# A branch hint for the jump past the general path, at the head of each engine's instructions

## The chip, the cores and the metric

The kernel runs on one core of one Trainium2 chip. The metric is the device time of one execution in microseconds (us); the number that counts is the median of several executions.

## What is computed

Two parts follow each other. The first is a gated linear attention over `B = 4` batches, `H = 8` heads, `S = 768` steps and head size `D = 48`, all in float32. Per head and step, with a state matrix of 48 by 48:

```
y[t]  = r[t] . (state + u * k[t] (x) v[t])
state = w[t] * state + k[t] (x) v[t]
```

The second takes the heads side by side as rows of 384 numbers and runs a gated block:

```
h = relu(x @ w_in)                      # 384 -> 1024
u, v = h[:, :512], h[:, 512:]
v_n = (v - mean(v)) / sqrt(var(v) + 1e-6)
v_s = w_spatial @ v_n + b_spatial       # over the 768 steps
out = (u * v_s) @ w_out                 # 512 -> 384
```

## The kernel before

The sequence is cut into chunks of 128 steps, six for each of the four batches, so 24 slots. In each slot decay products are formed by two scans on VectorE, the chunk's scores and outputs by matrix products on TensorE, and the state is carried to the next chunk. Behind each slot one normalised part of the gated block (`hv_unit`) runs, and behind each batch its gate and output parts (`g_unit`, `out_unit`). Products that must be exact to float32 are made of three passes over split operands (`mm3`, lines 582 to 584).

None of this is a loop on the chip: every instruction of the fast path is written out, which makes thousands for TensorE and some hundreds for each other engine. The order is written by hand. `PLAN` is a list of 1810 entries; each names an engine (T TensorE, V VectorE, A ScalarE, G GpSimd, S SyncE for the transfers) and an operation, and five entries (F) are idle matmuls that keep TensorE at work. `issue` (line 713) walks the list and issues each entry on its engine. Nothing on the chip decides about the order.

The chunked form divides by products of decays, so it holds only while these are not too small and no decay is above 1. `range_check` (lines 792 to 802) reduces that to one integer, `bad`, in the last entries of the plan. Behind the plan every engine loads `bad` from memory into a register (line 849), and a branch on each engine (line 850) decides: when `bad` is 1, a slow step by step form runs, `general()`, which lies in the program between the branch and the end; when it is 0, as with these inputs, every engine jumps past it. Behind the jump the engines clear their semaphores, meet, and end.

The last output tile is copied by ScalarE (line 708) and stored by a transfer that SyncE issues (line 710); it lies ahead of SyncE's load of `bad`.

## Time and profile before

| what | us |
|---|---|
| median of three runs | 373.29 |
| lowest and highest of them | 369.5 and 373.3 |
| the profiled execution, its own time | 369.84 |
| span of the profiled execution, first to last instruction | 368.0 |
| TensorE busy | 353.6 (96% of the span) |
| VectorE, ScalarE, GpSimd busy | 252.5, 176.6, 164.5 |

The profiled execution's own time is 1.8 us above its span. Of three runs one took 369.5 and two took 373.3, so an execution can differ from another by 1% with nothing changed, and the profiled one is of the short kind. In the profile PE is TensorE, PEld its weight loads, DVE VectorE, ACT ScalarE, POOL GpSimd and SP SyncE; a name with a q (SPq) is that engine's instruction queue, where register, branch, semaphore and transfer-issuing instructions run. Those are not counted as busy.

### The profile page before, as it was taken

How to read it: one execution, taken by the hardware profiler on the slowest of the kernel's cores; microseconds unless marked ns; L12 is line 12 of the kernel's file. 1: busy time of each engine (PE TensorE's matmuls, PEld its weight loads, DVE VectorE, ACT ScalarE, POOL GpSimd, SP SyncE). 2: the span in 40 equal slices, each digit the busy share in tenths (PEclk: the TensorE clock that was granted, in tenths of full speed). 3: DMA queues.
4: the chain of work that ended last, by engine and by line, in shares of the span. 5: the costliest groups of instructions: out<-in, count | busy, mean ns of one | idle time of the engine just before them, and what ended most of it. 6: DMA issues, size and time to landing. Idle time of an engine off the chain costs nothing.

```text
span 368.0 us, 9503 instructions
## 1 busy us (share of the span) xinstructions
PE 353.6 (96%) x3824; PEld 327.5 (89%) x3824; DVE 252.5 (69%) x475; ACT 176.6 (48%) x470; POOL 164.5 (45%) x211
## 2 busy tenths in 40 slices
PE   7897899999999999999999999999999999999992
PEld 7786688989998898999889999999899998999991
DVE  5989998979977986678756785885784562422240
ACT  3565778745334776614363856422256257303111
POOL 4878866446434753448644305265342220233030
PEclk9999989999999999999999999999999999999998
DMA  7988567822365447324355644242345101100102
GB/s 201 304 246 228 193 210 218 247 61 69 111 177 170 135 132 219 111 89 139 106 166 169 185 122 132 89 138 85 119 137 157 63 2 45 62 4 0 67 0 75
DMA packets 33013, 47.70 MB, mean 130 GB/s; under 512 B 3264, under 2 KB 21824, under 8 KB 32960
## 3 DMA queue, kind: packets, MB, share of 16 engines
q1 hardware_dynamic: 32960, 47.00, 43.2%
q8 instruction: 32, 0.52, 0.6%
q14 instruction: 21, 0.17, 0.1%
HBM read 42.27 MB, written 4.72 MB: 128 GB/s over the span
## 4 chain that ended last, share of the span: by engine, by line
PE 84%; DVE 7%; POOL 2%; issue 2%; DMA 1%; SPq 1%; ACT 0%; POOLq 0%; DVEq 0%; ACTq 0%
PE pyw L502 9%; PE pv L582 9%; PE pv L584 8%; PE pv L583 8%; PE pa L462 6%; PE po L582 5%; PE po L584 5%; PE po L583 5%; PE pu L582 4%; PE ph L582 4%; PE pu L584 4%; PE pu L583 4%; PE ph L583 4%; PE ph L584 4%; PE pd L540 2%; PE pt L482 2%
## 5 line engine op out<-in xcount | busy, mean ns | idle before, releaser
L582 PE MATMUL pv<-ws,vh 128*128 128x384 f32 x192 | 65.5, 341 | 0.0
L584 PE MATMUL pv<-ws,vl 128*128 128x384 f32 x192 | 64.5, 336 | 0.8 <-POOL vl L654 0.8
L583 PE MATMUL pv<-ws,vh 128*128 128x384 f32 x192 | 64.3, 335 | 0.0
L690 POOL TENSOR_TENSOR t<-t,us 128x384 f32<-128x384 f32 x21 | 22.7, 1088 | 56.1 <-DVE t L688 56.0
L467 DVE COPY_PREDICATED As<-mask,pa 128x512 f32<-128x512 int32 x48 | 34.5, 734 | 11.3 <-PE pa L462 5.6
L692 ACT CAST gh<-t 128x384 fp32r<-128x384 f32 x32 | 16.0, 511 | 48.5 <-POOL t L690 36.3
L688 DVE TENSOR_TENSOR t<-pv,b_sb 128x384 f32<-128x384 f32 x32 | 17.6, 553 | 28.6 <-PE pv L584 28.6
L582 PEld LDWEIGHTS pv<-ws,vh 128*128 128x128 f32 x192 | 36.1, 188 | 1.1 <-DVE prod L408 0.2
L584 PEld LDWEIGHTS pv<-ws,vl 128*128 128x128 f32 x192 | 36.0, 188 | 1.1 <-POOL vl L654 1.1
L583 PEld LDWEIGHTS pv<-ws,vh 128*128 128x128 f32 x192 | 36.1, 188 | 0.3
L443 POOL TENSOR_SCALAR_AFFINE_SELECT As<-dg 128x512 f32<-128x512 f32 x33 | 24.9, 762 | 23.9 <-DVE dg L428 10.9
L404 DVE TENSOR_TENSOR_SCAN F<-zz,W 112x512 f32<-112x512 f32 x24 | 29.2, 1218 | 8.6 <-ACT zz L416 6.5
L582 PE MATMUL pu<-xT,wi 128*128 128x384 f32 x96 | 33.1, 344 | 0.0
L582 PE MATMUL po<-wo,gh 128*128 128x384 f32 x96 | 33.1, 344 | 0.0
L584 PE MATMUL pu<-xT,wi 128*128 128x384 f32 x96 | 32.3, 337 | 0.0
L584 PE MATMUL po<-wo,gl 128*128 128x384 f32 x96 | 32.3, 337 | 0.0
L583 PE MATMUL po<-wo,gh 128*128 128x384 f32 x96 | 32.2, 336 | 0.0
L583 PE MATMUL pu<-xT,wi 128*128 128x384 f32 x96 | 32.2, 336 | 0.0
L462 PE MATMUL pa<-rr,kk 48*128 48x128 f32 x384 | 27.9, 284 | 3.1 <-POOL As L443 1.6
L654 POOL TENSOR_TENSOR vl<-hv,vh 128x512 fp32r<-128x512 f32 x14 | 20.7, 1484 | 22.2 <-ACT vh L652 11.9
L582 PE MATMUL ph<-wi,xT 128*128 128x512 f32 x72 | 29.7, 413 | 0.6 <-DVE S L548 0.6
L412 DVE TENSOR_TENSOR_SCAN pa<-zz,W 112x512 f32<-112x512 f32 x24 | 29.3, 1222 | 0.3
(182 smaller groups left out, 842.6 us busy)
## 6 DMA issues: line engine op xcount, KB each, us to landing
N<-in_nat_dram SPq DMA_DIRECT2D x18, 384.0 KB, 3.4
Nw<-in_gt_dram SPq DMA_DIRECT2D x16, 384.0 KB, 3.4
W<-in_tr_dram SPq DMA_DIRECT2D x24, 224.0 KB, 3.4
kk<-in_tr_dram SPq DMA_DIRECT2D x24, 224.0 KB, 4.0
rr<-in_tr_dram SPq DMA_DIRECT2D x24, 224.0 KB, 3.7
v<-in_nat_dram SPq DMA_DIRECT2D x24, 192.0 KB, 2.9
out_dram<-ot SPq DMA_DIRECT2D x24, 192.0 KB, 1.9
wst<-in_w_spT_dram SPq DMA_DIRECT2D x12, 192.0 KB, 4.3
```

What stands on the lines that cost most here:

```text
L404: op({"V": 1.24}, lambda: nc.vector.tensor_tensor_scan(flat(F()[:R])[:, ::-1], flat(zz[:R])[:, ::-1], flat(W())[:, ::-1], 0.0, ALU.max, AL ...
L412: op({"V": 1.24}, lambda: nc.vector.tensor_tensor_scan(flat(E()[:R]), flat(zz[:R]), flat(W()), 0.0, ALU.max, ALU.mult), r=[(W, 0), ("zz", ...
L443: e.affine_select(out=As(), in_=dg()[:, j::2].unsqueeze(2).broadcast_to([P, G, C]), pattern=[[0, G], [1, C]], compare_op=ALU.is_equal, fil ...
L462: nc.tensor.matmul(pa[j]()[:, g, :], kk()[rs, g, :], rr()[rs, g, :], start=True, stop=True)
L467: op({"V": 0.725}, lambda j=j, As=As: nc.vector.copy_predicated(As(), mask.unsqueeze(1).broadcast_to([P, G, C]), pa[j]()), r=[(pa[j], 0)], ...
L502: nc.tensor.matmul(py()[Q * n:Q * (n + 1), k_, :], a, b, start=n not in started, stop=not left[0], skip_group_check=True)
L582: nc.tensor.matmul(ps, ah, bh, start=first, stop=False)
L583: nc.tensor.matmul(ps, ah, bl, start=False, stop=False)
L584: nc.tensor.matmul(ps, al, bh, start=False, stop=last)
L654: lambda e, hv=hv, vh=vh, vl=vl: e.tensor_tensor(vl(), hv(), vh().bitcast(F32), ALU.subtract),
L688: op({"V": dve(HT)}, lambda: nc.vector.tensor_tensor(t1(), pv()[:, :HT], b_sb[:, tsl], ALU.add), r=[(pv, 0), ("b", 0)], w=[(t1, 0)])
L690: op({"V": dve(HT), "G": pool(HT)}, lambda e: e.tensor_tensor(t1(), t1(), us(), ALU.mult), r=[(us, 0)], w=[(t1, 0)], port=True)
```

## The change

A constant `HINT = 400` is added. `issue` is given a position in the plan, `len(plan) - HINT`, and when it comes there it marks, for all engines, a hint for the branch labelled `past`, with the word that it is likely taken. The branch at line 850 is given that label. A hint is an instruction that names a branch and says which way it will go; it computes nothing. In the program as built, the hint of each engine stands among that engine's first instructions, not at the place in the plan. Nothing else is added, removed or moved: the branch stays, and so do the check, the plan and the general path.

```
+HINT = 400
...
-    def issue(order):
-        for o in order:
+    def issue(order, mark=None):
+        for n, o in enumerate(order):
+            if n == mark:
+                tc.mark_branch_hint_location("past", "LikelyTaken", engines=list(mybir.ALL_ENGINES))
             if isinstance(o, int):
                 warm(o)
...
         plan = prog.plan()
-        issue(plan)
+        issue(plan, len(plan) - HINT)
     att.close()
     rv = nc.values_load(bad[0:1, 0:1], min_val=0, max_val=1)
-    with tc.If(rv > 0):
+    with tc.If(rv > 0, label="past"):
         general()
```

## Rows read from the trace of the kernel before

**Rows 1.** Busy time by stretch: start:end, length, then each engine's busy us (instructions), clock, transfers.

```profile
100.00:200.00 100.00, 100.00 (x1251) 91.80 (x1250) 75.70 (x141) 50.79 (x143) 52.41 (x67) 1.00 0.50 144
300.00:355.00 55.00, 55.00 (x357) 53.76 (x357) 17.88 (x35) 16.79 (x40) 12.82 (x14) 1.00 0.08 30
...
361.36:368.03 6.67, 0.00 (x0) 0.00 (x0) 0.00 (x0) 0.00 (x0) 0.00 (x0) 0.86 0.19 66
```

**Rows 2.** The chain that ended last, from 361.3 us on: start, length, what.

```profile
360.87 0.48 ACT ot L708
```

**Rows 3.** Line 849, the load of the flag: engine, count, duration min/median/max ns, first and last start.

```profile
L849 ACTq TENSOR_LOAD <-bad x1: 617/617/617, 361.1 to 361.1; - x1
...
L849 SPq TENSOR_LOAD <-bad x1: 506/506/506, 361.8 to 361.8; - x1
L849 SPq FUSED_REGOPS  x1: 183/183/183, 362.3 to 362.3; - x1
```

**Rows 4.** Line 850, the branch, and what each engine runs next behind it.

```profile
L850 SPq EVENT_SEMAPHORE  x8: 17/17/17, 366.1 to 366.7; - x8
L850 ACTq COMPARE_BRANCH  x1: 50/50/50, 361.8 to 361.8; - x1
L850 POOLq COMPARE_BRANCH  x1: 45/45/45, 361.8 to 361.8; - x1
L850 DVEq COMPARE_BRANCH  x1: 72/72/72, 361.9 to 361.9; - x1
L850 PEldq COMPARE_BRANCH  x1: 3800/3800/3800, 361.9 to 361.9; - x1
L850 SPq COMPARE_BRANCH  x1: 50/50/50, 362.6 to 362.6; - x1
L850 POOLq EVENT_SEMAPHORE  x1: 17/17/17, 365.5 to 365.5; - x1
L850 ACTq EVENT_SEMAPHORE  x1: 17/17/17, 365.7 to 365.7; - x1
L850 PEldq EVENT_SEMAPHORE  x1: 51/51/51, 365.7 to 365.7; - x1
L850 DVEq EVENT_SEMAPHORE  x1: 21/21/21, 365.8 to 365.8; - x1
```

**Rows 5.** Transfers by queue, 362.8 to 364.5 us: packets, megabytes, share of 16 engines.

```profile
q14 instruction: 4, 0.03, 6.3%
q8 instruction: 1, 0.02, 5.1%
```

**Rows 6.** Waits of SyncE's queue from 355 us on: us in total, times, longest.

```profile
SPq L850 <- SPq L850: 3.4, 1, 3.4
SPq L904 <- PEq L904: 0.6, 2, 0.5
```

**Rows 7.** Line 904, the meeting of the engines at the end.

```profile
L904 SPq EVENT_SEMAPHORE  x10: 17/28/28, 366.7 to 368.0; - x10
```

**Rows 8.** Line 710 from 359 us on: the last three stores of output.

```profile
L710 SPq DMA_DIRECT2D out_dram<-ot x3: 332/332/332, 359.8 to 361.4; - x3
...
DMA to landing us min/median/max: 1.9/1.9/1.9
```

**Rows 9.** The program's start, line 897, register moves and the engines' first meeting.

```profile
L897 SPq MOVE  x4: 29/34/42, 0.0 to 0.2; - x4
...
L897 SPq EVENT_SEMAPHORE  x1: 17/17/17, 0.7 to 0.7; - x1
```

**Rows 10.** The chain that ended last, 0 to 45 us, some of its longest pieces.

```profile
4.23 0.43 SPq L359
...
5.65 5.00 DMA kk<-in_tr_dram
...
27.31 1.21 DVE pa L412
...
33.47 1.69 issue
```

**Rows 11.** The whole page: transfers by queue, as in rows 5, over the span.

```profile
q8 instruction: 32, 0.52, 0.6%
q14 instruction: 21, 0.17, 0.1%
```

**Rows 12.** Busy time by stretch, as in rows 1, 45 to 49 us.

```profile
45.00:49.00 4.00, 4.00 (x20) 3.17 (x12) 3.97 (x6) 3.45 (x12) 2.14 (x5) 0.57 0.79 253
```

## The prediction

> **What bounds the kernel now.** I read the busy time by stretch first. From 100 us on TensorE is busy in every microsecond, at the full clock, down to 355 us, and the other engines have time to spare [rows 1]. So nothing that an engine other than TensorE saves or loses in that long middle shows at the end. What is open are the two ends. The last stretch is the odd one: from the end of the last busy instruction, ScalarE's copy of the last output tile at 360.87 + 0.48 = 361.35 us [rows 2], to the end of the span there are 6.67 us in which no engine computes at all [rows 1]. That tail is where the changed branch lies, so I took it apart by source line.

> Four engines load the flag at 361.1 us, SyncE only at 361.8, because its load stands behind its issue of the last store at 361.4 [rows 3, 8]. The four branch at 361.8 to 361.9 us, SyncE at 362.6. The branch itself is over in 45 to 72 ns on every engine but TensorE, whose record runs on for 3800 ns. Then the reader is to see the hole: the next instruction of any engine starts at 365.5 (GpSimd), 365.7 (ScalarE, TensorE), 365.8 (VectorE) and 366.1 (SyncE) [rows 4]. That is 3.6 to 3.9 us after the branch for four engines, and the waits of SyncE's queue give 3.4 us for it, with nothing to blame but its own line [rows 6]. What moves in that hole is in the transfers: four packets on one instruction queue and one on the other, 8 KB and 16 KB each (0.03 MB by four, 0.02 MB by one), so one block for each of five engines, and all behind the branches [rows 5]. The engines jump to code that they don't hold, and wait while it is brought.

> SyncE is last. It clears eight semaphores from 366.1 to 366.7, waits for the others from 366.7 and the end comes at 368.0 [rows 4, 7]: 1.9 us of work behind the hole, and it stays whatever the hint does.

> **The change, part by part.** It adds one hint per engine, and it may take away the hole. Nothing else moves.

> *The hole, if the target block is there when the branch comes.* SyncE decides, since it branches 0.7 us behind the others. Its wait of 3.4 us [rows 6] shrinks to what a jump to held code costs. No row shows one. From below it is the branch record itself, 0.05 us [rows 4]; from above I take the costliest thing in SyncE's queue that has to go to memory, its load, 0.51 us [rows 3]. The nearest row is the step from one of its eight waits to the next, (366.7 − 366.1) / 7 = 0.09 us [rows 4]; I take 0.1. Gain 3.4 − 0.1 = 3.3 us, between 2.9 and 3.35.

> *What is late next.* Without the hole SyncE would begin its eight waits near 362.75 us. The last store was issued at 361.4 and such stores land 1.9 us after issue [rows 8], at 363.3. One of the eight waits is for it. Were it the first, it would cost 363.3 − 362.75 = 0.55 us; the queue's waits take 0.09 each, so as the last of eight it would cost nothing (362.75 + 0.63 = 363.38). Rows don't tell which; I take the middle, 0.3. The other four engines would be through at 362.2 or so, ahead of SyncE, so the meeting at the end waits for nobody new. Left: 3.3 − 0.3 = 3.0 us.

> *The hint instructions.* One on each engine, with a register move or two at most. If they stand ahead of the engines' first meeting at 0.7 us, which SyncE reaches early and waits for [rows 9], they are hidden: 0. If behind it, SyncE's come ahead of its first transfers, and the chain of the first microseconds goes through its issues and the transfer of `kk` [rows 10]; no cover there. A move takes 0.03 us [rows 9], the longest register operation 0.18 [rows 3]. So 0 to 0.2, taken at 0.1. Below nothing is excluded for the instruction itself.

> Sum against the profiled execution: 369.84 − 3.0 + 0.1 = 366.9 us, with ends of 369.84 − 3.35 = 366.5 and 369.84 − 3.4 + 0.51 + 0.2 = 367.15 (a slow jump covers the store's landing). That execution is 3.45 us under the median of the runs, near the lowest. Nothing in this change speaks for either level, and the long runs have no trace here, so I put the same 2.9 us on the median: 373.29 − 2.9 = 370.4 us, 0.8% less. A measurement of this kernel can tell about 1% from no change; the whole hole, 3.4 us, is 0.9%. Whatever the hint does at the end, by itself it lies within that.

> **The rivals.**

> *The same gain, but the runs fall on the low level.* One of three runs before, and the profiled one, were at 369.5 to 369.8. Then the median is 369.5 − 2.9 = 366.6 us, 1.8% under the median of before. What makes the levels isn't in the trace of one run. [...] This is a coin toss with the weight a little on the median's side.

> *The hint does nothing.* It stands at the head of the program, and the branch at its end. If a hint fetches its target at once and the engine keeps only few blocks, the target is long gone by 361.8 us: over the span 32 and 21 instruction blocks are brought [rows 11], of which five are those of the hole [rows 5]. Then the same hole stays and only the hints' 0 to 0.2 us are added: 370.0 by the profiled execution, 373.4 on the median, or 369.6 if the runs fall low. For it: the distance. Against it: the hint names a branch, and an engine that keeps that name can fetch the target when it nears the branch, wherever the hint stood.
> [...]

> *Slower: the hinted block takes the place of one that is needed.* If each engine brings the target at the start and drops the next block in line for it, it stops at its first block boundary for a fetch like that at the end, 3.4 to 3.9 us [rows 4, 6]. TensorE could swallow some of it early, but VectorE and SyncE are on the chain of the first 45 us, with a wait there already that nothing explains, 1.69 us [rows 10]. The target is dropped again before the end, so the hole stays: 369.84 + 3.6 + 0.1 = 373.5 by the profiled execution, 373.29 + 3.7 = 377.0 on the median, 1.0% slower. It decides if an engine that is on the chain meets its boundary ahead of 100 us; behind that TensorE's busy stretch [rows 1] hides a stop of another engine.

> *Only some engines are helped.* If one of the four still fetches, it resumes at 365.8 as now [rows 4], and the meeting behind it takes the time from 366.7 on less SyncE's own waits, some 0.9 us: an end near 366.7 instead of 368.0, a gain of 1.3, so 372.0. If SyncE isn't helped, nothing is gained.

> **How the numbers follow.** Gain with the runs at the median's level: 0.40, 370.4 us. Gain at the low level: 0.34, 366.6. No effect: 0.15, 369.6 to 373.4. Some engines: 0.05, 372.0 or 368.2. Slower: 0.06, about 377. The range reaches from the low level with the largest gain, 369.5 − 3.35 = 366.2 us, to no effect at the high level with the dearest hints, 373.5; only the slower case is left out, but without the upper end of no effect about 2 in 10 would be. Faster by over 1% (under 369.6): the low-level case and a small part of the others, 0.37. Slower by over 1%: most of the slower case, 0.05. Within 1%: the rest, 0.58.

> **What the changed profile would show.** If the hint works, the first instruction of SyncE behind the branch starts about 0.1 us after it, the wait of 3.4 us is gone from its queue, the five instruction packets lie ahead of the branches, and the tail of 6.67 us is near 3.6. If it does nothing, the hole and the packets stay where they are. If it displaces a block, waits without a releaser of over 3 us stand in the first 100 us. I am wrong in the large if the tail is unchanged, or if the start, which a hint may shift, moves by more than the tail gives.

## The result, and the profile after

Over 22 executions the changed kernel has a median of 366.82 us (365.77 to 373.18), the kernel before one of 373.26 (368.54 to 375.45), so the medians are 1.7% apart. The ratio of 0.9882, with a 95% interval of 0.9844 to 0.992, is not that of these medians but is taken over the executions of each kernel that lie within 1.5% of its fastest alone (16 after, 18 before): 1.2% faster, give or take 0.4.

The executions of either kernel fall into two groups by time, which go with TensorE's mean granted clock (in the changed kernel 0.986 or more in the group of shorter times, 0.982 or less in that of longer ones), and the median of 22 lies in the upper group of times before (9 executions of 368.5 to 370.8, 13 of 372.7 to 375.5) and in the lower one after (14 of 365.8 to 367.3, 8 of 370.6 to 373.2). Group against group the change is 369.36 to 366.46 us, 2.9 less, and 373.74 to 371.51, 2.2 less. So some 2.9 us (0.8%) are the hint's where the clock held, and the rest of the 6.4 us between the medians is which group they fall in. How much that can be is seen in 29 more executions of the kernel before, run beside the experiments: their median is 370.50 us, with 15 of 368.6 to 370.5 (clock 0.988 or more) and 14 of 373.1 to 376.1 (0.978 or less). Nothing was changed, and the median moved by 2.8 us. Whether the hint has a part in how often an execution falls into the longer group isn't shown: 27 of 51 did before, 8 of 22 after.

Line 850 is line 854 now, 849 is 853, 904 is 908, 710 is 712. The branch, and what each engine runs next, in the changed kernel (columns as in [rows 4]):

```profile
L854 SPq EVENT_SEMAPHORE  x8: 17/17/17, 363.6 to 364.1; - x8
...
L854 PEldq COMPARE_BRANCH  x1: 388/388/388, 362.3 to 362.3; - x1
L854 ACTq EVENT_SEMAPHORE  x1: 17/17/17, 362.7 to 362.7; - x1
L854 POOLq EVENT_SEMAPHORE  x1: 17/17/17, 362.8 to 362.8; - x1
L854 PEldq EVENT_SEMAPHORE  x1: 51/51/51, 362.8 to 362.8; - x1
L854 DVEq EVENT_SEMAPHORE  x1: 21/21/21, 362.9 to 362.9; - x1
L854 SPq COMPARE_BRANCH  x1: 70/70/70, 363.1 to 363.1; - x1
```

The waits of SyncE's queue from 350 us on, of the same kernel:

```profile
SPq L908 <- PEq L908: 0.6, 2, 0.5
SPq L854 <- SPq L854: 0.4, 1, 0.4
```

The hole is gone from all five engines. Four branch at 362.3 us and go on 0.4 to 0.6 us later, where [rows 4] showed 3.6 to 3.9. TensorE's branch record has shrunk from 3800 to 388 ns. SyncE branches at 363.1 and goes on at 363.6; its wait of 3.4 us [rows 6] is 0.4 now. The tail, the stretch behind ScalarE's last copy, as busy time by stretch [rows 1]:

```profile
361.81:365.52 3.71, 0.00 (x0) 0.00 (x0) 0.00 (x0) 0.00 (x0) 0.00 (x0) 1.00 0.29 104
```

It was 6.67 us and is 3.71, 2.96 less. The instruction queues of the whole page, against [rows 11]:

```profile
q8 instruction: 31, 0.51, 0.6%
q14 instruction: 17, 0.14, 0.1%
```

q8 moved 0.51 MB in 31 packets and q14 0.14 MB in 17, so blocks of some 16 and 8 KB. I take q8 for TensorE's and q14 for that of the other four: with the hint on SyncE alone, below, q14 brings one block less, with the hint on the other four three less. So it is one block less for TensorE and four less for the others, one per engine. What is missing is missing behind the branches: ahead of them both kernels bring 30 and 13 blocks. Behind them the kernel before brings ten (360 to 369 us):

```profile
q14 instruction: 8, 0.07, 2.4%
q8 instruction: 2, 0.03, 1.7%
```

and the changed one five (361.9 to 365.5 us):

```profile
q14 instruction: 4, 0.03, 3.1%
q8 instruction: 1, 0.02, 1.6%
```

Before, five of the ten come in the hole, and five more from 366.1 us on, when the engines have gone on; only such a second five are left after, from 363.3 us on. So as many blocks come ahead of the branches as before, 30 and 13, and the five that came in the hole do not come. No view shows what a block holds; that the target is now among the blocks ahead, in the place of one that the jump leaves unused, is my inference from these counts. The hints themselves stand at 0.8 to 0.9 us, behind the first meeting, and take 45 to 51 ns (line 908, the hint of each engine, first and last):

```profile
L908 POOLq BRANCH_PREFETCH_HINT  x1: 48/48/48, 0.8 to 0.8; - x1
...
L908 PEldq BRANCH_PREFETCH_HINT  x1: 50/50/50, 0.9 to 0.9; - x1
```

The profiled execution takes 367.33 us, 2.51 less than that of before (369.84); the tail gives 2.96 of it, and 0.45 were lost ahead of the tail, of which the hints explain about 0.1: SyncE issues its first transfer at 0.92 us instead of 0.81. The other 0.35 is less than what executions of one group differ by (365.8 to 367.3).

### The profile page after: what moved, and what is told of

It reads as the page before. It is cut to its first block, busy times and chain, and to the rows that moved or that the text cites. A ratio compares the mean times of both kernels' runs of the same rounds, so it can differ in the third digit from the quotient of the medians.

```text
span 365.5 us, 9508 instructions
## 1 busy us (share of the span) xinstructions
PE 353.8 (97%) x3824; PEld 327.7 (90%) x3824; DVE 257.2 (70%) x475; ACT 176.8 (48%) x470; POOL 163.4 (45%) x211
## 4 chain that ended last, share of the span: by engine, by line
PE 80%; DVE 9%; DMA 3%; POOL 3%; issue 2%; ACT 1%; SPq 0%; DVEq 0%; POOLq 0%; ACTq 0%
PE pv L584 9%; PE pv L586 8%; PE pv L585 8%; PE pyw L504 8%; PE pa L464 6%; PE po L584 5%; PE po L586 5%; PE po L585 5%; PE pu L584 4%; PE pu L586 4%; PE pu L585 4%; PE ph L584 4%; PE ph L586 4%; PE ph L585 3%; PE pt L484 2%
## 5 line engine op out<-in xcount | busy, mean ns | idle before, releaser
L464 PEld LDWEIGHTS pa<-rr,kk 48*128 48x128 f32 x384 | 23.4, 187 | 7.0 <-issue 3.4
```

Source lines behind the costliest of these rows:

```text
L464: nc.tensor.matmul(pa[j]()[:, g, :], kk()[rs, g, :], rr()[rs, g, :], start=True, stop=True)
```

## The experiments

All ends are measured from the issue of the last store, since what lies ahead of it moves with the clock from one execution to the next (in the traces with a mean clock of 0.986 or more that store is issued at 360.4 to 361.8 us, in those with 0.980 or less at 364.6 to 366.7). From the traces, in us (differences taken before rounding):

| kernel | last store issued | span ends | difference |
|---|---|---|---|
| before | 361.38 | 368.03 | 6.65 |
| the change | 361.83 | 365.52 | 3.69 |
| hint on SyncE alone | 361.74 | 367.14 | 5.41 |
| hint on the other four | 366.71 | 373.32 | 6.61 |
| hints just ahead of the load | 364.92 | 371.64 | 6.72 |
| short general path, no hint | 365.87 | 368.85 | 2.99 |
| hints 140 us into the kernel | 360.53 | 364.08 | 3.55 |
| hints 255 to 260 us in | 360.42 | 366.99 | 6.57 |
| no range assertion | 361.38 | 364.90 | 3.53 |
| no assertion, last store by ScalarE | 361.55 | 365.17 | 3.62 |
| no branch at all | 366.18 | 369.12 | 2.93 |
| the change, six more idle matmuls | 364.64 | 368.32 | 3.69 |

The theory to be tested: each engine jumps to code that it doesn't hold and fetches it; its own hint makes it bring that block ahead of its branch. The rivals: the added instructions shift the code, or the fetches hinder each other, or a taken branch is dear in any case.

**The hint on SyncE alone.**

```
-                tc.mark_branch_hint_location("past", "LikelyTaken", engines=list(mybir.ALL_ENGINES))
+                tc.mark_branch_hint_location("past", "LikelyTaken", engines=[mybir.EngineType.SP])
```

> The hint on SyncE alone. Counted from the issue of the last store, the end of the span came 6.65 us later before and 3.69 after the change. Theory (each engine fetches the block it jumps to, and its own hint brings that block ahead of its own branch): SyncE's next instruction starts 0.5 us after its branch, the other four still wait 3.6 to 3.9 us for their blocks and meet SyncE late, so the end comes about 5.4 us after the issue of the last store: a gain of 1.2 us. Rival (the added instructions only shift the code so that the targets fall into blocks already held, on every engine or on none): 3.7 or 6.65 us.

Line 854 in this kernel, SyncE's branch and what follows on VectorE, and the waits of SyncE's queue:

```profile
L854 SPq EVENT_SEMAPHORE  x8: 17/17/17, 363.5 to 364.0; - x8
...
L854 SPq COMPARE_BRANCH  x1: 70/70/70, 363.0 to 363.0; - x1
...
L854 DVEq EVENT_SEMAPHORE  x1: 21/21/21, 366.1 to 366.1; - x1
```

```profile
SPq L908 <- DVEq L854: 1.8, 1, 1.8
```

SyncE goes on after 0.5 us, the others wait as before, and SyncE now stands 1.8 us for VectorE. The end comes at 5.41, as the theory had it (about 5.4); code that only shifts would have given 3.7 or 6.65. The hint works engine by engine (0.5 us on the engine that had it, 3.5 to 3.9 on those that had not), and the engine that goes on last sets the price.

**The hint on the other four.** The same line with every engine but `SP`.

> The hint on the four engines other than SyncE. Theory: the four go on 0.4 to 0.6 us after their branches, SyncE waits 3.4 us as before, and since it is last the end comes 6.65 us after the issue of the last store, no gain at all. Rival (the five fetches hinder each other, so that fewer of them are shorter): SyncE's wait shrinks to 2.5 us or less and the end comes at 5.7 us or earlier.

The waits of SyncE's queue in this kernel:

```profile
SPq L854 <- SPq L854: 3.4, 1, 3.4
```

The four go on by 367.8 us after branches at 367.1 to 367.2; SyncE waits 3.4 us as before. The end comes at 6.61. So four hints out of five are worth nothing if the one that is missing is SyncE's. The rival is not settled by this: the four others still bring a block each behind their branches, at 368.2 to 368.4 us, and SyncE's own follows at 368.9, so it has as many beside it as before. What a fetch with none beside it would cost isn't shown.

**All hints just ahead of the load of the flag.** With `HINT = 400` the hints stood at 0.8 to 0.9 us, at the head of the program as built, and not 400 entries from the end; so the load, the hint and the branch went into a block of their own.

```
+    with tc.block():
+        tc.mark_branch_hint_location("past", "LikelyTaken", engines=list(mybir.ALL_ENGINES))
-    rv = nc.values_load(bad[0:1, 0:1], min_val=0, max_val=1)
+        rv = nc.values_load(bad[0:1, 0:1], min_val=0, max_val=1)
...
```

> All five hints, but in a block of their own behind the whole plan, just ahead of the load of the flag. Theory (the block is fetched from the hint on, if the branch is near): SyncE's hint comes some 1.2 us ahead of its branch, so of the 3.4 us about 2.2 stay, and the end comes 5.2 to 5.6 us after the issue of the last store. Rival (what counts is that the instruction is there, not when): 3.7 us as with the hint at the head.

Both were wrong. Line 910 holds the hints of this kernel, line 856 the branches:

```profile
L910 POOLq BRANCH_PREFETCH_HINT  x1: 48/48/48, 357.3 to 357.3; - x1
L910 PEldq BRANCH_PREFETCH_HINT  x1: 45/45/45, 361.4 to 361.4; - x1
...
L910 SPq BRANCH_PREFETCH_HINT  x1: 50/50/50, 365.3 to 365.3; - x1
```

```profile
L856 PEldq COMPARE_BRANCH  x1: 507/507/507, 365.4 to 365.4; - x1
L856 PEldq EVENT_SEMAPHORE  x1: 51/51/51, 366.0 to 366.0; - x1
...
L856 POOLq EVENT_SEMAPHORE  x1: 17/17/17, 369.1 to 369.1; - x1
```

**Hints in the middle of the plan.** The hint was put ahead of the 1000th and, in a second kernel, the 400th entry from the end, with its word taken from a register. So written it stood where that register is loaded: at 140.2 to 143.9 us in the first, at 255.2 to 260.5 in the second.

```
+    way_sb = cp.tile([1, 1], I32, name="way")
+    nc.gpsimd.memset(way_sb, 0)
...
-                tc.mark_branch_hint_location("past", "LikelyTaken", engines=list(mybir.ALL_ENGINES))
+                way = nc.values_load(way_sb[0:1, 0:1])
+                tc.mark_branch_hint_location("past", way, engines=list(mybir.ALL_ENGINES))
```

> All five hints ahead of the thousandth entry from the end of the plan, about 140 us into the kernel, each behind a load of a zero into a register that says the branch will be taken (0.5 to 0.7 us on each queue, some of it shown by TensorE). Theory (a hint works if it stands ahead of the moment at which the engine brings the block behind the one that holds its branch): seven blocks are still to come on the small instruction queue behind that point, so all five engines go on 0.4 to 0.6 us after their branches and the end comes 3.6 to 3.8 us after the issue of the last store. Rival (a hint works from the head of the program alone): 6.65 us.

> The same with the hints ahead of the 400th entry from the end, where the change meant to put them, about 270 us into the kernel. In the trace of before only two blocks of the small instruction queue are brought behind that point, at 287.9 and 346.6 us. Theory: of ScalarE, VectorE, GpSimd and SyncE at most two are helped, by the count of instructions ScalarE and VectorE; TensorE is; GpSimd and SyncE wait 3.4 to 3.9 us as before, and the end comes 6.6 us after the issue of the last store. Rival (a hint may stand anywhere but close to its branch): 3.7 us.

Transfers on the instruction queues from 262 us to the branch in the second:

```profile
q8 instruction: 7, 0.11, 0.5%
q14 instruction: 2, 0.02, 0.0%
```

and line 857, the branch and what follows, in the second:

```profile
L857 SPq EVENT_SEMAPHORE  x8: 17/17/17, 365.1 to 365.6; - x8
...
L857 ACTq EVENT_SEMAPHORE  x1: 17/17/17, 361.3 to 361.3; - x1
L857 PEldq EVENT_SEMAPHORE  x1: 51/51/51, 361.4 to 361.4; - x1
L857 SPq COMPARE_BRANCH  x1: 70/70/70, 361.4 to 361.4; - x1
L857 DVEq EVENT_SEMAPHORE  x1: 21/21/21, 361.5 to 361.5; - x1
L857 POOLq EVENT_SEMAPHORE  x1: 17/17/17, 364.8 to 364.8; - x1
```

Only two blocks were still to come for the four engines, and exactly two of them were helped, the two that were named: ScalarE and VectorE. GpSimd and SyncE waited 4.0 and 3.6 us, and the end came at 6.57, as if there were no hint. With the hints at 140 us, ahead of seven such blocks, all five engines went on 0.5 to 0.6 us after their branches and the end came at 3.55, a little under the forecast. Here a hint served 220 us ahead of its branch as it did at the head; 100 us ahead was too late for GpSimd and SyncE.

The blocks brought on q14 over the whole span agree with the theory kernel by kernel. They were 21 without a hint; with the hint on SyncE alone, on the other four (three of them on this queue), and at 255 to 260 us (two helped) they were

```profile
q14 instruction: 20, 0.16, 0.1%
q14 instruction: 18, 0.15, 0.1%
q14 instruction: 19, 0.16, 0.1%
```

and with the hints just ahead of the load, which helped none of the four, 21 again: one block less for each engine helped, no less for the others.

**A short general path, no hint.** The branch leads past one instruction and not past the whole slow form (the kernel has no second way for inputs out of range).

```
     with tc.If(rv > 0):
-        general()
+        nc.vector.memset(zk, 0.0)
```

> No hint, but the general path cut to one memset on VectorE, so that the code jumped to lies right behind the branch (the kernel then has no second way for inputs out of range). Theory (the wait is for code that is far away): the waits behind the branches are gone as with the hint, 0.3 to 0.6 us, and the end comes 3.5 to 3.8 us after the issue of the last store. Rival (a taken branch by itself costs 3.4 us, wherever it goes): 6.65 us as before.

Line 850 in this kernel:

```profile
L850 DVEq COMPARE_BRANCH  x1: 72/72/72, 365.6 to 365.6; - x1
...
L850 PEldq COMPARE_BRANCH  x1: 223/223/223, 365.7 to 365.7; - x1
L850 DVEq EVENT_SEMAPHORE  x1: 21/21/21, 365.9 to 365.9; - x1
```

The next instruction comes 0.2 us after the branch, on TensorE 0.3, with a record of 223 ns, against 3.4 to 3.9 us behind the branches that lead past the general path [rows 4, 6]. Here it isn't the branch that is dear but the distance. The end, 2.99, can't be compared with the forecast: in this kernel as built SyncE issues its last store behind the branch, so branch and load lie ahead of the store. Only the waits can, and they are gone.

**What is left.** Two kernels take work off SyncE behind the hint: one without the range assertion, one also with the last store issued by ScalarE. A third has no load and no branch (it checks and doesn't act on it).

```
-    rv = nc.values_load(bad[0:1, 0:1], min_val=0, max_val=1)
+    rv = nc.values_load(bad[0:1, 0:1])
...
-        op({"S": 0.45}, lambda: nc.sync.dma_start((out[b] if dst is None else dst)[t0:t0 + C, :], ot()),
+        op({"S": 0.45}, lambda: (nc.scalar if (b, h, j) == (B - 1, 1, NH - 1) else nc.sync).dma_start(
+            (out[b] if dst is None else dst)[t0:t0 + C, :], ot()),
```

> The changed kernel without the range assertion on the loaded flag, which SyncE works on between its load and its branch. Theory (SyncE's queue sets the end): the end comes 3.25 to 3.35 us after the issue of the last store, 0.4 us sooner than with the hint alone. Rival (the store's landing sets it by now): 3.7 us, no change.

> The changed kernel, with the last store issued by ScalarE right behind its own copy, and without the range assertion on the loaded flag. With the hint, SyncE is still last: its load of the flag stands behind its last store, and its queue works 0.43 us on the assertion. Theory: SyncE loads the flag with the others, branches 0.8 us earlier, and the end comes 2.6 to 3.0 us after the issue of the last store, against 3.69 with the hint alone and 6.65 before; against the kernel before 3.7 to 4.0 us less between executions whose clock fell alike. Rival (the landing of the last store is next, 1.9 us after its issue, with 1.2 us of clearing and meeting behind it): 3.1 us or more, so 0.6 us or less beyond the hint.

> The kernel before without the flag's load, the branch and the general path (the check is computed, nothing comes of it). This is the floor for any hint: what remains behind the last store is its landing and the meeting of the engines. Theory: the end comes 2.6 to 3.0 us after the issue of the last store, so the whole check costs 3.7 to 4.0 us before and 0.7 to 1.0 us with the hint. Rival (a part of the tail is the ordinary end of any program): 3.6 us as with the hint, which would then hide all of it.

Without the assertion the end came at 3.53, 0.16 sooner instead of 0.4; with ScalarE's store at 3.62, where 2.6 to 3.0 had been expected. The waits of SyncE's queue in the kernel with ScalarE's store:

```profile
SPq L855 <- SPq L855: 1.3, 2, 0.9
```

The jump is one of the two waits, 0.4 us; the other is 0.9 us long, ahead of the fourth of the eight semaphores, taken to be that of the last store, which ScalarE issued at 361.55: cleared at 363.51, 1.96 us later. So behind the hint the landing of the last store is the next limit, as the rival said, and all but 0.2 us of what SyncE can save runs into it. Over 12 executions that kernel had a median of 366.92 us (ratio to before, taken as above, 0.9939, interval 0.9892 to 0.9987), no better than the change alone; in the group of the higher clock 366.7 against 366.5.

Without any branch the end came at 2.93, and 10 executions had a median of 368.28 us (ratio 0.9928, interval 0.987 to 0.9986; five in each clock group, 365.6 and 370.5). The whole acting on the check cost 6.65 − 2.93 = 3.7 us before, and 0.8 with the hint: the hint hides four fifths of it, and nothing tried here hides more than 0.2 us of the rest.

**More idle matmuls at the start.** Six more, in the plan's first hundred entries.

```
-S56 G17 G32 A1c V19 G48 S57 A15 F2 T4m V49 G45 G4d S5 V1a V4a T1d T1e S1p T46 A1f S58 V4n Sc V4b V4e A4c T4j G4g
+S56 G17 G32 A1c V19 G48 S57 A15 F4 T4m V49 G45 G4d S5 V1a V4a T1d T1e S1p T46 A1f S58 V4n Sc V4b V4e A4c F4 T4j G4g
```

> The changed kernel with six more idle matmuls on TensorE, two and four of them ahead of two operations for which it waits 0.5 to 0.8 us between 10 and 13.3 us. In three of the traces so far the granted clock fell to half for 13.7 us from 15.6 to 16.3 us on, in three it did not. If those waits bring the fall about, all executions come out near 366.5 us and none near 371.5. If they don't, executions are spread over both as before, and each is 0 to 0.5 us longer.

What the two clock groups are is seen by setting the kernel with four hints against the changed one, busy time by stretch, first the one with four hints:

```profile
16.30:29.90 13.60, 13.04 (x145) 10.99 (x149) 9.52 (x16) 6.49 (x15) 7.50 (x8) 0.50 0.60 179
```

```profile
16.30:29.90 13.60, 12.03 (x246) 10.39 (x247) 13.03 (x22) 8.78 (x22) 11.27 (x12) 1.00 0.88 264
```

For 13.6 us the granted clock is 0.50 in the one and 1.00 in the other; TensorE starts 145 matmuls in the one and 246 in the other, though it is busy 13.0 us of the stretch in the one and 12.0 in the other. Ahead of it, from 12 to 16.2 us, both had a clock of 1.00; TensorE waited 0.8, 0.5 and 0.6 us between 10 and 17 us in the one that fell, 0.5 and 0.6 in the one that didn't. The same fall, 13.65 us long, stands in all five traces of executions in the longer group, whose mean clock is 0.974 to 0.980 (in four from 15.6 to 16.6 us on), and in none of the seven others, with 0.986 to 0.995. With the added matmuls the waits in that stretch were 0.3 and 0.6 us (four of the six ran behind the operation whose wait they were meant to fill), and in the profiled execution the clock held at 16 us and fell at 28.9 instead, for as long. Of 12 executions three were still in the lower clock group, which can't be told from 8 of 22, and the median of all is 367.63 us (ratio 0.9927, interval 0.9889 to 0.9965). The nine others have a median of 367.3, 0.9 us above the changed kernel's 366.5, where 0 to 0.5 had been expected. So the fall is not removed, and in the one execution with a trace it came later. What decides it in one execution and not in the next isn't settled.

## Why the prediction was right, and where not

The time, 366.82 us, lies in the range, and the direction was right; the likeliest case was not the one that came. I put 370.4 us on it, the gain with the runs at the median's level, and what came was the second case, the same gain at the low level, forecast at 366.6. That the medians fell into different clock groups I had as a toss with the weight on the wrong side.

- *The hole.* Right in kind: without the hint one block per engine comes in the hole [rows 5] and the engines stand 3.4 to 3.9 us, with it none of these comes and they stand 0.4 to 0.6. The size was off: from branch to next instruction SyncE needs 0.50 us, not 0.1. I took the step from one wait to the next as the nearest row; the upper bound, 0.51, was near the value. Part of it is shown by the short path, where near code costs 0.2; what the other 0.3 is isn't shown. Gain at this step 3.0 us, not 3.3. The sign that I gave, five instruction packets ahead of the branches, doesn't show as such: five still come behind them, but by the counts above they are the second five of the ten of before.
- *What is late next.* I took 0.3 us for the landing of the last store. It cost nothing: the eight waits follow each other without a gap from 363.6 to 364.1. In the three kernels in which a gap stands among the eight (without the assertion, with ScalarE's store, with the hints at 140 us) it stands ahead of the fourth, which is cleared 1.87 to 1.96 us after the store's issue; so neither the first nor the last of the eight is the store's, but the fourth. In the changed kernel SyncE comes to the fourth at 363.86, 2.03 us after the issue. The two errors are one: the jump is 0.4 us dearer, and by then the store has landed; with a jump of 0.1 the fourth would have been reached near 363.46 and have waited some 0.3, as taken (an estimate from these times). That the landing is next was right: the two kernels that save time on SyncE run into it at once.
- *The hints.* 45 to 51 ns each, behind the first meeting; SyncE's first transfer is issued 0.1 us later, as taken.
- *The sum.* Tail 2.96 us shorter, forecast 3.0. Against the clock group of the profiled execution 2.9, forecast 2.9; the profiled execution itself came at 367.33, not 366.9, since it lost 0.45 us ahead of the tail.
- *The clock and the levels.* What makes the levels I left open. A fall at 45 us is in both profiles, before [rows 12] and after (0.57 over the same 4 us), and both are of the group of shorter times. What goes with the group of longer times is another fall, 13.65 us long, in four of five traces from about 16 us, which neither of the two has.
- *The hint does nothing.* This fell. The hint at 0.8 to 0.9 us still counted at the branches at 362.3 to 363.1, with 30 and 13 blocks brought ahead of them: five blocks are brought less, and no engine waits over 0.6 us. How many blocks an engine keeps is not measured here.
- *Slower, by a displaced block.* Not seen: the changed kernel has no wait of over 3 us without a cause in its first 100 us; the longest such wait is 1.1.
- *Only some engines are helped.* Confirmed by hand: SyncE alone gives 5.41, a gain of 1.24, against the 1.3 that I had worked out; the others alone give nothing.

## What to carry to other kernels

A jump over a long stretch of code cost each engine here a wait of 3.4 to 4.0 us for a fetch, and at the end of a kernel the engine that goes on last sets what is paid; look at the start of the first instruction behind a branch, not at the branch's own record, which was over in 45 to 72 ns on four of the five. A hint at the head, or 220 us ahead of the branch, left 0.4 to 0.6 us of that wait on each engine; 100 us ahead it came too late for two engines, 0.9 to 8 us ahead TensorE alone had its block in time. One engine left out can keep the whole price: 6.61 us without SyncE's hint, 6.65 without any. When two medians differ by more than the stretch that was changed, sort the executions by their granted clock before believing the difference.

## What the runs showed that was not expected

- On four engines no fetch was seen to follow a hint: with two blocks still to come on their queue exactly two of them were helped, with none no block came ahead of a branch, even 8 us ahead. On TensorE, hinted 4 us ahead, a block came 1.0 us after the hint and the wait was 0.6 us.
- A hinted branch past the general path cost 0.4 to 0.6 us, a branch past one instruction without a hint 0.2 to 0.3.
- Kernels with the same first 30 us ran these at full clock in some executions and 13.6 us of them at half in others, and the two groups of times lie 4.4 us apart before and 5.0 after.
